# Attention's maxima: split and transposed by VectorE in blocks of 32x32, where TensorE and ScalarE did it through a bank of PSUM

## The chip, the cores and the metric

The kernel runs on one core of one Trainium2 chip. The metric is the device time of one execution in microseconds. The engines are named as the profile names them: PE (TensorE; PEld are its weight loads), DVE (VectorE), ACT (ScalarE), POOL (GpSimd) and SP (SyncE, which only issues DMAs here).

## The reference

One transformer block on a sequence of 2048 rows of 576 values, all in float32. The modulation vectors come from a small product with the condition `c`. The step that matters is attention with 32 heads of 18 values each:

```python
def _A_ref(x, wqkv, wo):
    B, S, D = x.shape
    H = 32; Dh = D // H
    qkv = (x @ wqkv).reshape(B, S, 3, H, Dh).transpose(2, 0, 3, 1, 4)
    q, k, v = qkv[0], qkv[1], qkv[2]
    scores = jnp.einsum("bhqd,bhkd->bhqk", q, k) * Dh ** -0.5
    p = _softmax(scores, axis=-1)
    o = jnp.einsum("bhqk,bhkd->bhqd", p, v)
    return o.transpose(0, 2, 1, 3).reshape(B, S, D) @ wo
```

Around it stand layer norms with modulation, and after it a gated feed-forward part, `(sigmoid(h @ w_gate) * (h @ w_up)) @ w_down` with 4608 hidden values. The inputs `A_wqkv` and `A_wo` are drawn eight times larger than the others, so that the scores are large and the softmax needs the true maximum of each row.

## The kernel before, in words

**Stages.** The first 270 us or so normalise the rows and project queries, keys and values. Then comes attention, up to about 1540 us, with other work woven into it (the weights of the feed-forward part, the output projection of finished rows). The rest is the feed-forward part. The change lies in attention.

**Numbers in two parts.** Products run on values that are split into a high part, which the PE reads exactly (type float32r), and a low part that holds the rest. A query or key head of 18 values therefore takes 54 rows of a tile: high, low and high once more. Two heads lie in one tile, at rows 0 and 64.

**Units and steps.** Attention is 32 units. A unit is two heads and one half of the queries (1024 columns in the tile `q0`, `q1` or `q2`, taken in turn). A unit has 16 steps `kt`, one for each block of 128 keys. In a step the PE makes four blocks of transposed scores (L1084: 128 keys by 512 queries, for two heads and two column halves), ACT takes the exponential of each (L1088), and two steps later the PE multiplies them by the values (L656).

**The maxima.** The exponential needs the maximum of each query's scores. It enters the product as two more rows of the query tile: under the 54 rows of head h stand rows 54 and 55 (64 h + 54 and 64 h + 55), the high and the low part of the negated maximum, and the key tile has ones there. So L1084 reads 56 rows, and the maximum is subtracted inside the product. The maxima are computed about one and a half units ahead: generator `maxima()` makes scores once more with queries on the partitions (L550, 54 rows), in 64 turns for a unit, and DVE reduces each block (L556). Of eight blocks one is passed by ACT through a Relu into `over` (L559) and joined with the next by DVE (L561). After the last turn of a unit, L568 reduces the parts to `nm`, 128 queries by 16 (two heads by 8 blocks of 128 queries), negated.

**Spread.** `nm` has a query on each partition, but the two rows of the query tile have them along one partition. `spread(qs, nm)` carries them over: the PE transposes `nm` into a bank (L581: 16 by 128), ACT copies the bank to float32r, which is the high part (L585), DVE subtracts it from the bank, which gives the low part (L586), and four DMAs on SP (L590) write the rows, one for each head and part, in eight pieces of 512 bytes each. `spread` is a generator: up to its `yield` it issues the transpose, after it the rest.

**Banks.** All scores, transposes and other results in attention take turns in seven banks of PSUM (`bank()`), so an instruction of the PE waits until the reader of the result seven places earlier is done.

**The order of the work.** For PE and ACT the order is written by hand: the context `manual_schedule` names both, and they run in the order of the code. It follows the strings in `STEPS`, one for each pair of steps: `t0` and `t1` are blocks of scores for the exponential (head 0 or 1), `m0`, `m1`, `r0` and `x0` are turns of the maxima (`r0` goes to the Relu, `x0` joins), `V` is a whole product with the values, `A` and `B` its halves, `K` takes a finished output, `O`, `S` and `G` are places where other work starts, and `c` continues what was started. A pair uses the entry of its step number, or `half`; in units 15 to 27 and a half it uses `rows`. Entry 12 is the one with an `S`. When the ninth turn of the next unit's maxima comes, `state["spread"]` is set; that is in the pair at `kt` 12, and the spread then starts at the pair's `S` (or `G`) and goes on at its `c`. The spread of the first unit lies in the projections. DVE, POOL and SP are put in order by the framework's planner: it walks through the program with its own estimate of durations, takes for each engine the first instruction in the order of the code that is ready, and may so put a later one ahead. Within an engine the order is then fixed.

**SP.** On its queue stand, in this part of the program, the DMAs of the spread and the loads of queries and keys for a later unit (`load_heads`, L514 to L522), which are issued at the start of a unit. The maxima of the next unit must have landed in the query tile before that unit's first `L1084`.

Of the kernel before, what the change touches and what calls it, by code (L numbers as in the profile page):

```python
# [23 lines left out]
P = 128  # L24
# [34 lines left out]
}  # L59
ORDERED = 7  # L60
SEVENS = NB - 2
# [26 lines left out]
def tile_block(ctx, tc, x_in, wqkv, wo, w_gate, w_up, w_down, c_in, w_mod, out):  # L88
# [437 lines left out]
    def maxima():  # L526


        n = HW // P
        last = None  # L530
        for u in range(UNITS):
            qs, ks = heads(u)
            mx = mxs[u % 2]
            if u not in SINGLE and u - 2 in SINGLE:
                nc.gpsimd.memset(mx[:, 0:n, 1], LOWEST)
            for i in range(8 * n):
                if last is not None and i == (9 if u == 1 else 8):
                    if u == 1:
                        for _ in spread(*last):
                            pass  # L540
                    else:
                        state["spread"] = last
                qt = i // 8
                pairs = u not in SINGLE
                h, kc = state.get("at") or MAXIMA[i % 8]
                rows = slice(64 * h, 64 * h + 3 * DH)
                paired = pairs and h == 0 and kc < 2
                at = NCH if paired and kc == 0 else kc
                sp = bank()
                nc.tensor.matmul(  # L550
                    sp, qs[rows, qt * P : (qt + 1) * P],
                    ks[rows, at * 512 : (at + 1) * 512], start=True, stop=True,
                )
                to = mx[:, h * n + qt, kc : kc + 1]
                if not paired:
                    nc.vector.tensor_reduce(to, sp, axis=AX.X, op=ALU.max)  # L556
                elif kc == 0:
                    over = small.tile([P, 512], F32, name="over", bufs=1)
                    nc.scalar.activation(over, sp, AF.Relu)  # L559
                else:  # L560
                    nc.vector.tensor_tensor_reduce(  # L561
                        out=over, in0=sp, in1=over, scale=1.0, scalar=LOWEST,
                        op0=ALU.add, op1=ALU.max, accum_out=mx[:, h * n + qt, 0:1],
                    )
                if i < 8 * n - 1:
                    yield
            nm = small.tile([P, 2, n], F32, name="nm")
            nc.vector.tensor_reduce(  # L568
                nm.rearrange("p h t -> p (h t)"), mx, axis=AX.X, op=ALU.max, negate=True
            )  # L570
            last = (qs, nm)
            yield
        for _ in range(8):
            yield
        state["spread"] = last

    def spread(qs, nm):

        n = HW // P
        tp = bank()[0 : 2 * n, 0:P]  # L580
        nc.tensor.transpose(tp, nm.rearrange("p h t -> p (h t)"), ident)  # L581
        yield
        mrows = small.tile([32 + 2 * n, P], F32R, name="mrows", bufs=1)
        parts = [mrows[32 * l : 32 * l + 2 * n] for l in range(2)]
        nc.scalar.copy(parts[0], tp)  # L585
        nc.vector.tensor_sub(parts[1], tp, parts[0].bitcast(F32))  # L586
        for h in range(2):
            for l, part in enumerate(parts):
                to = 64 * h + 3 * DH + l
                nc.sync.dma_start(  # L590
                    qs[to : to + 1, :].rearrange("l (t q) -> l t q", q=P).bitcast(F32),
                    part[n * h : n * (h + 1), :].bitcast(F32),
                )

    todo = maxima()
# [443 lines left out]
    for u in range(UNITS):  # L1039
# [6 lines left out]
        for kt in range(NT):  # L1046
            step = u * NT + kt
            turns["to"] = 64 + 4 * LEAD + 8 * (step // 2 + 1)
            kcols = slice(kt * P, (kt + 1) * P)
            if kt % 2 == 0:  # L1050
                heavy = state.get("next") == "g"
                hold = heavy and (kt == 2 or kt == 12 and u < UNITS - 1)
                halved = step >= 10 and (hold or not heavy)
                rows = FROM0 <= step < FROM1
                order = two_steps(STEPS["full" if not halved else "rows" if rows else kt if kt in STEPS else "half"])
            probs = [None] * 4
            for does, h, c in order[kt % 2]:
                if does == "m":
                    turn(h, c)
                elif does == "K":  # L1060
                    taken()
                elif does in "OSG":
                    if halved and kt == 2:
                        follow.append(outputs())
                        next(follow[-1], None)
                    if "spread" in state:
                        follow.append(spread(*state.pop("spread")))
                        next(follow[-1])
                    if does == "G" and step >= FROM0 and not hold:
                        state["next"] = next(rows0 if step < FROM1 else rows1, None)  # L1070
                elif does == "c":
                    for _ in range(len(follow)):
                        work = follow.pop(0)
                        if next(work, "done") != "done":
                            follow.append(work)
                elif does == "V":
                    if step >= LAG:
                        values()
                elif does in "AB":
                    values(slice(0, 256) if does == "A" else slice(256, 512))  # L1080
                else:
                    sT = bank()
                    rows = slice(64 * h, 64 * h + 3 * DH + 2)
                    nc.tensor.matmul(  # L1084
                        sT, ks[rows, kcols], qs[rows, c * 512 : (c + 1) * 512], start=True, stop=True
                    )
                    pr = probs[2 * c + h] = ppool.tile([P, 512], F32, name=f"p{2 * c + h}")
                    state["exp"] = nc.scalar.activation(pr, sT, AF.Exp, scale=SCALE)  # L1088
            pending.append((half, p, kt, probs))
            if u in (1, 3):  # L1090
                if kt == 0:
                    a = big.tile([P, 8, 640], F32, name="big")
                    a = a.rearrange("p a b -> p (a b)")[:, 0 : 8 * D].rearrange("p (t c) -> p t c", t=4)
                    b = slots.tile([P, 2560], F32, name="w0")[:, 0 : 2 * D]
                    mods = load_mod(a, b, 1 + u // 2)
                    row = slots.tile([P, 2560], F32, name="w1")[:, 0:544]
                    weighed = weigh(mods)
                elif kt >= 5:
                    next(weighed, None)
            elif u in (2, 4) and kt in (2, 4):  # L1100
                takes = [(ga_b, None), (mcol2[:, 1, :], 0.0)] if u == 2 else [(mcol2[:, 0, :], 1.0), (gb_b, None)]
                if kt == 2:
                    weighed = modulate(row, mods[:1], HALVES, takes)
                next(weighed, None)
            if 4 * NT + 8 <= step < FROM0 and step % 4 != 3:
                next(downs, None)
            if step == FROM0:
                for _ in downs:
                    pass
            if step == FROM1 - 1:  # L1110
                for _ in rows0:
                    pass
                bgs.close()
                rawst = ExitStack()
                raws = rawst.enter_context(tc.tile_pool(name="raws", bufs=1, side="right"))
            if u == 30 and kt == 7:
                first = [load_block(raws, b, k, paced) for b, k in ((0, 0), (0, 1), (1, 1))]
            if u >= 30 and kt == 2:
                load_x(u - 30, f"k{u - 30}")
            if u == UNITS - 1 and kt == 3:  # L1120
                nc.sync.dma_start(oend[:, :, 0 : D - DL - 2 * DH], Os[1][:, :, DL : D - 2 * DH])
            if u == UNITS - 1 and kt == 9:
                for _ in rows1:
                    pass
                load_x(2, "w0")
                load_x(3, "w1")
                both = big.tile([P, 2, 5, 512], F32R, name="big")
                for i in range(2):
                    X[5 + i] = both[:, i]
                    load_x(5 + i)  # L1130
# [687 lines left out]
```

## Time and profile before

| | us |
|---|---|
| median of the runs (3 runs, 2797.94 to 2798.35) | 2798.32 |
| the profiled execution | 2804.88 |
| span of its instructions | 2803.1 |
| attention, units 0 to 14 (about) | 267 to 831 |
| attention, units 15 to 31 (about) | 831 to 1540 |

A row of the groups reads: line, engine, operation, what it writes and reads, shapes and count, then durations. In the timeline the first number is the start in us, the second the time taken, and the brackets give the idle time before the instruction and what ended it. `PEld` rows are weight loads; the load of a product waits for what the product waits for, so its start tells when the PE could go on. In the table by stretches each row has the stretch, its length, and the busy time of PE, PEld, DVE, ACT and POOL with the count of instructions, then PE's granted clock, the busy share of the DMA engines, and GB/s.

### The profile page before, as it was taken

What the parts mean: (1) busy time and instruction counts of PE and PEld (TensorE: products, weight loads), DVE (VectorE), ACT (ScalarE), POOL (GpSimd) and SP (SyncE); (2) the same over time, 40 slices, a digit from 0 to 9 for tenths busy, and PEclk for the clock granted to TensorE, in tenths of its full rate; (3) what the DMA queues carried; (4) which work ended last, traced back from release to release, by engine and by line L of the source; (5) the groups of instructions that cost most, each with busy time, mean ns of one, the idle gap of its engine ahead of it and who ended that gap; (6) DMA issues with size and microseconds to landing.
All of it is one profiled execution on the core that took longest, in us unless ns stands there. A gap on an engine that the chain in (4) does not pass through costs nothing.

```text
span 2803.1 us, 50644 instructions
## 1 busy us (share of the span) xinstructions
PE 2771.9 (99%) x18637; PEld 1847.4 (66%) x18637; DVE 2306.3 (82%) x4370; ACT 1609.3 (57%) x3051; POOL 814.6 (29%) x1077
## 2 busy tenths in 40 slices
PE   7999999999999999999999999999999999999999
PEld 5975444444444444444444888888888888888888
DVE  7278999999998888999883778888898677777777
ACT  3215999999999878999888332333333222222221
POOL 3125207888843111663103222232221100000000
PEclk9999999999999999999999999999999999999999
DMA  5344224444432120232127766667767956566653
GB/s 172 121 157 140 78 61 162 171 169 166 172 133 82 36 58 24 98 106 71 43 68 227 273 222 223 240 213 273 278 245 280 339 195 201 194 200 195 200 195 120
DMA packets 170777, 462.59 MB, mean 165 GB/s; under 512 B 21212, under 2 KB 88032, under 8 KB 160416
## 3 DMA queue, kind: packets, MB, share of 16 engines
q1 hardware_dynamic: 150064, 360.72, 38.4%
q0 software_dynamic: 20464, 98.62, 9.9%
q8 instruction: 147, 2.41, 0.4%
q14 instruction: 102, 0.84, 0.1%
HBM read 281.92 MB, written 176.82 MB: 164 GB/s over the span
## 4 chain that ended last, share of the span: by engine, by line
PE 92%; DVE 4%; DMA 2%; issue 2%; POOL 0%; ACT 0%; SPq 0%; DVEq 0%; ACTq 0%; POOLq 0%
PE x L1225 26%; PE o L656 19%; PE s L1084 12%; PE s L550 11%; PE d L1375 8%; PE d L1307 6%; PE s L336 4%; PE s L805 2%; PE s L389 1%; DMA out_dram<-Oa 1%; DVE mx L556 1%; PE s L683 1%; DMA wq_raw<-in_A_wqkv_dram 1%; DVE w L1215 0%; DVE Oa L1379 0%
## 5 line engine op out<-in xcount | busy, mean ns | idle before, releaser
L1088 ACT ACTIVATE p<-s 128x512 f32<-128x512 f32 x2048 | 1069.1, 616 | 89.2 <-PE s L1084 62.6
L556 DVE TENSOR_REDUCE mx<-s 128x1 f32<-128x512 f32 x1568 | 1000.9, 683 | 101.3 <-PE s L550 75.1
L656 PE MATMUL o<-p,vaug 128*32 128x256 f32 (+1 forms) x5848 | 595.1, 478 | 0.1
L550 PE MATMUL s<-k,q 54*128 54x512 f32 x1920 | 548.6, 434 | 2.0 <-DVE t L775 1.0
L1084 PE MATMUL s<-q,k 56*128 56x512 f32 x1920 | 527.7, 440 | 0.0
L550 PEld LDWEIGHTS s<-k,q 54*128 54x128 f32 x1920 | 273.4, 184 | 231.9 <-DVE mx L561 88.0
L1084 PEld LDWEIGHTS s<-q,k 56*128 56x128 f32 x1920 | 249.8, 184 | 232.1 <-ACT p L1088 72.9
L1225 PE MATMUL x<-k,w 128*128 128x512 f32 x1512 | 370.0, 392 | 0.0
L1225 PEld LDWEIGHTS x<-k,w 128*128 128x128 f32 x1512 | 276.8, 188 | 53.3 <-PE o L656 0.8
L1375 PE MATMUL d<-wd,hh 128*128 128x288 f32 x1248 | 249.9, 295 | 2.4 <-DVE Oa L1379 2.4
L656 PEld LDWEIGHTS o<-p,vaug 128*32 128x32 f32 x5848 | 116.2, 108 | 203.1 <-issue 187.5
L1225 PE MATMUL x<-big,w 128*128 128x512 f32 x1008 | 245.5, 392 | 0.7 <-DVE u L1724 0.7
L1225 PE MATMUL x<-w,w 128*128 128x512 f32 x1008 | 245.3, 391 | 0.0
L1225 PEld LDWEIGHTS x<-big,w 128*128 128x128 f32 x1008 | 185.1, 188 | 37.0 <-DVE u L1724 1.1
L1225 PEld LDWEIGHTS x<-w,w 128*128 128x128 f32 x1008 | 184.3, 188 | 34.5
L1375 PEld LDWEIGHTS d<-wd,hh 128*128 128x128 f32 x1248 | 202.2, 188 | 6.2 <-DVE Oa L1379 3.1
L1375 PE MATMUL d<-wd,hl 128*128 128x288 f32 x624 | 184.3, 295 | 0.0
L1379 DVE TENSOR_TENSOR Oa<-Oa,d 128x288 f32<-128x288 f32 x312 | 136.6, 453 | 55.1 <-PE d L1375 51.2
L561 DVE CUSTOM_DVE_ANT_0 over<-s,over 128x512 f32<-128x512 f32 x240 | 163.9, 683 | 1.3 <-PE s L1084 1.2
L559 ACT ACTIVATE over<-s 128x512 f32<-128x512 f32 x240 | 145.8, 608 | 11.3 <-PE s L550 9.3
L1234 ACT ACTIVATE sg<-x 128x512 f32<-128x512 f32 x36 | 21.6, 599 | 210.2 <-PE x L1225 210.2
L1206 ACT CAST w<-S 128x768 fp32r<-128x768 f32 x71 | 59.4, 836 | 137.8 <-POOL S L1179 136.0
(275 smaller groups left out, 3898.5 us busy)
## 6 DMA issues: line engine op xcount, KB each, us to landing
ws<-w SPq DMA_DIRECT2D x126, 640.0 KB
w<-ws SPq DMA_DIRECT2D x126, 640.0 KB
wd<-wds SPq DMA_DIRECT2D x19, 1152.0 KB
k<-kd SPq DMA_DIRECT2D x60, 360.0 KB
wds<-w POOLq DMA_DIRECT2D x18, 1152.0 KB, 5.2
wtd<-t POOLq DMA_DIRECT2D x32, 576.0 KB, 5.0
wt<-wtd SPq DMA_DIRECT2D x64, 288.0 KB
wd<-wds SPq DMA_DIRECT2D x52, 288.0 KB
```

The source lines that it names most:

```text
L336: nc.tensor.matmul(acc, w, hT[:, t, cols], start=n == 0, stop=n == len(ts_) - 1)
L550: nc.tensor.matmul(sp, qs[rows, qt * P : (qt + 1) * P], ks[rows, at * 512 : (at + 1) * 512], start=True, stop=True,)
L556: nc.vector.tensor_reduce(to, sp, axis=AX.X, op=ALU.max)
L559: nc.scalar.activation(over, sp, AF.Relu)
L561: nc.vector.tensor_tensor_reduce(out=over, in0=sp, in1=over, scale=1.0, scalar=LOWEST, op0=ALU.add, op1=ALU.max, accum_out=mx[:, h * n + q ...
L656: nc.tensor.matmul(acc[32 * j : 32 * j + 32, cols], vaug[:, kt, (2 * p + h) * VW : (2 * p + h) * VW + 32], probs[2 * c + h][:, cols], star ...
L1084: nc.tensor.matmul(sT, ks[rows, kcols], qs[rows, c * 512 : (c + 1) * 512], start=True, stop=True)
L1088: state["exp"] = nc.scalar.activation(pr, sT, AF.Exp, scale=SCALE)
L1225: nc.tensor.matmul(acc[v], w[:, v, a, :], X[s][:, b, :], start=first and n == 0, stop=n == 6, skip_group_check=not first,)
L1307: nc.tensor.matmul(acc, a[:, rows], w[:, k, :], start=n == 0, stop=n == 2)
L1375: nc.tensor.matmul(acc[:, :HALF], a[:, f, rows], w[:, f, cols], start=n == 0, stop=n == 5)
L1379: nc.vector.tensor_add(Oa[:, t, cols], Oa[:, t, cols], acc[:, :HALF])
```

## The change

`spread` no longer uses the PE, ACT or a bank. DVE copies `nm` into the high part of a tile `split` (128 by 32: head, part, block) and subtracts it for the low part, then transposes `split` in four separate blocks of 32 by 32 into `mrows`. In block `a` (partitions 32 a to 32 a + 31) the rows are head, part and block of 128 queries, and the 32 columns are the queries 32 a to 32 a + 31 of each block. Eight DMAs, one for each block `a` and head, write both rows of the head: 2 by 8 pieces of 128 bytes each. `spread` is now a plain function that issues everything at one place, the pair's `G`; the entry for `kt` 12 in `STEPS` and the letter `S` are gone, so that pair takes the usual order `half`.

```diff
@@ STEPS
-    12: "V t0m1 m0t1 m1t0 S A c r0t1 m1t0 G B c t1t0 m1x0 t1m0",
@@ maxima()
                 if last is not None and i == (9 if u == 1 else 8):
                     if u == 1:
-                        for _ in spread(*last):
-                            pass
+                        spread(*last)
@@ spread(qs, nm)
         n = HW // P
-        tp = bank()[0 : 2 * n, 0:P]
-        nc.tensor.transpose(tp, nm.rearrange("p h t -> p (h t)"), ident)
-        yield
-        mrows = small.tile([32 + 2 * n, P], F32R, name="mrows", bufs=1)
-        parts = [mrows[32 * l : 32 * l + 2 * n] for l in range(2)]
-        nc.scalar.copy(parts[0], tp)
-        nc.vector.tensor_sub(parts[1], tp, parts[0].bitcast(F32))
-        for h in range(2):
-            for l, part in enumerate(parts):
-                to = 64 * h + 3 * DH + l
+        split = small.tile([P, 4 * n], F32R, name="split", bufs=1)
+        hi, lo = (split.rearrange("p (h l t) -> p h l t", h=2, l=2)[:, :, l, :] for l in range(2))
+        nc.vector.tensor_copy(hi, nm)
+        nc.vector.tensor_sub(lo, nm, hi.bitcast(F32))
+        mrows = small.tile([P, 4 * n], F32R, name="mrows", bufs=1)
+        nc.vector.transpose(mrows.bitcast(F32), split.bitcast(F32))
+        for a in range(4):
+            for h in range(2):
+                to, p0 = 64 * h + 3 * DH, 32 * a + 2 * n * h
                 nc.sync.dma_start(
-                    qs[to : to + 1, :].rearrange("l (t q) -> l t q", q=P).bitcast(F32),
-                    part[n * h : n * (h + 1), :].bitcast(F32),
+                    qs[to : to + 2, :].rearrange("l (t a q) -> l t a q", a=4, q=32)[:, :, a, :].bitcast(F32),
+                    mrows[p0 : p0 + 2 * n, :].bitcast(F32),
                 )
@@ the loop over units and steps
-                elif does in "OSG":
+                elif does in "OG":
                     ...
                     if "spread" in state:
-                        follow.append(spread(*state.pop("spread")))
-                        next(follow[-1])
+                        spread(*state.pop("spread"))
```

## The prediction

> **What bounds the kernel now.** I read the page first, then the busy time of each engine over single pairs of attention steps, then the starts of TensorE's weight loads, then VectorE, SyncE and the lines of the edit.
>
> ```profile
> span 2803.1 us, 50644 instructions
> PE 2771.9 (99%) x18637; PEld 1847.4 (66%) x18637; DVE 2306.3 (82%) x4370; ACT 1609.3 (57%) x3051; POOL 814.6 (29%) x1077
> ```
>
> The average says TensorE and nothing else. The edit lies in attention alone, so I cut four neighbouring pairs out of unit 12, from one Relu to the next; the columns are length, then busy time of PE, PEld, DVE, ACT and POOL. Below them stand the two halves of attention.
>
> ```profile
> 719.35:723.98 4.63, 4.63 (x42) 2.05 (x40) 4.35 (x9) 4.54 (x11) 4.63 (x8) 1.00 0.28 116
> 723.98:728.61 4.63, 4.63 (x42) 2.00 (x40) 4.39 (x10) 4.56 (x11) 4.55 (x8) 1.00 0.00 0
> 728.61:733.44 4.83, 4.83 (x43) 2.03 (x41) 4.68 (x9) 4.72 (x11) 4.83 (x9) 1.00 0.31 126
> 733.44:738.20 4.76, 4.76 (x42) 2.02 (x40) 4.49 (x10) 4.52 (x11) 3.52 (x6) 1.00 0.81 286
> ...
> 267.00:831.00 564.00, 564.00 (x4781) 242.12 (x4779) 524.11 (x991) 548.38 (x1099) 341.19 (x534) 1.00 0.40 138
> 831.00:1500.00 669.00, 666.00 (x5316) 295.90 (x5314) 583.35 (x1130) 592.76 (x1179) 203.62 (x278) 1.00 0.22 68
> ```
>
> In the first half all three engines are nearly full: in an ordinary pair of 4.63 us ACT works 4.54 to 4.56 and DVE 4.35 to 4.39, which leaves DVE 0.24 to 0.28 us. In the second half DVE idles 669.00 - 583.35 = 86 us. So an instruction taken from ACT or PE should show in the first half, and one given to DVE is not free there.
>
> **What the step costs now.** These are weight loads at the first score of each pair, in unit 12 with the transpose's own load, and of three pairs in unit 21, the last with the transpose.
>
> ```profile
> 721.95 0.18 PEld L1084 LDWEIGHTS s<-q,k 56*128 56x128 f32 x1 [0.84 <-ACT p L1088]
> 726.56 0.18 PEld L1084 LDWEIGHTS s<-q,k 56*128 56x128 f32 x1 [0.84 <-ACT p L1088]
> 731.23 0.18 PEld L1084 LDWEIGHTS s<-q,k 56*128 56x128 f32 x1 [0.84 <-ACT p L1088]
> 732.13 0.09 PEld L581 LDWEIGHTS s<-ident,nm 128*16 128x16 f32 x1 [0.25 <-issue]
> 736.20 0.18 PEld L1084 LDWEIGHTS s<-q,k 56*128 56x128 f32 x1 [0.84 <-ACT p L1088]
> ```
>
> ```profile
> 1109.12 0.18 PEld L550 LDWEIGHTS s<-k,q 54*128 54x128 f32 x1 [0.18 <-ACT p L1088]
> 1113.80 0.18 PEld L550 LDWEIGHTS s<-k,q 54*128 54x128 f32 x1 [0.18 <-ACT p L1088]
> 1118.63 0.18 PEld L550 LDWEIGHTS s<-k,q 54*128 54x128 f32 x1 [0.20 <-ACT p L1088]
> ```
>
> Unit 12: two pairs of 4.61 and 4.67 us, mean 4.64, then the pair with the transpose, 736.20 - 731.23 = 4.97: an excess of 0.33 us. Unit 21: 4.68, then 4.83: an excess of 0.15. There are 32 spreads. One lies in the projections; 15 lie in units 0 to 14, and 16 in units 15 to 30.
>
> **Removed.** The group rows of the four instructions (duration lowest, median, highest in ns):
>
> ```profile
> L581 PE MATMUL s<-ident,nm x32: 276/277/278, 215.9 to 1487.3; 128*16 128x128 f32 x32
> L585 ACT CAST mrows<-s x32: 237/239/256, 216.2 to 1488.7; 16x128 fp32r<-16x128 f32 x32
> L586 DVEq EVENT_SEMAPHORE  x60: 49/50/50, 269.4 to 1485.2; - x60
> L586 DVE TENSOR_TENSOR mrows<-s,mrows x32: 279/280/283, 216.7 to 1488.9; 16x128 fp32r<-16x128 f32 x32
> L590 SPq DMA_DIRECT2D q<-mrows x128: 620/630/1506, 216.5 to 1491.0; - x128
> ```
>
> The excess of 0.33 us is what 0.28 of PE, 0.24 of ACT and the DVE subtraction cost together; they overlap, so I take the measured excess and not their sum. The special order goes too, and the pair is then ordered as its three predecessors, whose 4.64 us is what I measure against. Gain if nothing came in place: 15 x 0.33 = 5.0 and 16 x 0.15 = 2.4, together 7.4 us. The bank that the transpose took is free as well; that is inside the excess.
>
> **Added on VectorE.** Copy, subtract and transpose, over 16, 16 and 32 elements, each needing the one before. No row shows a DVE transpose or a copy this small. The nearest rows are small dependent operations in attention:
>
> ```profile
> 1079.38 1.28 DVE L556 TENSOR_REDUCE mx<-s 128x1 f32<-128x512 f32 x2
> 1080.58 0.16 DVE L228 TENSOR_SCALAR sd<-sd 128x8 f32<-128x8 f32 x1
> 1080.65 0.68 DVE L561 CUSTOM_DVE_ANT_0 over<-s,over 128x512 f32<-128x512 f32 x1
> ...
> 1082.05 0.17 DVE L226 TENSOR_TENSOR sd<-r 128x8 f32<-128x8 f32 x1
> 1082.25 0.17 DVE L227 TENSOR_TENSOR sd<-sd,var 128x8 f32<-128x8 f32 x1
> 1082.45 0.17 DVE L228 TENSOR_SCALAR sd<-sd 128x8 f32<-128x8 f32 x1
> ```
>
> Alone between two big reductions such an operation moves the next one by 0.07 us (1080.65 - 1080.58). In a chain each takes 0.20 us (1082.05, 1082.25, 1082.45). So three cost 0.21 us at least and 0.60 at most. Against DVE's 0.24 us of room the lower end costs the pair nothing, and the upper 0.36. The Trainium skill ("VectorE: DVE Perf Modes", section "Rules for kernel authors") says that chaining VectorE operations saves nothing and that their number should be kept small; that speaks against one operation becoming three. By it the sum would take the chain's end; the row with 0.07 us disagrees with it where a long reduction stands on either side.
>
> Which end applies depends on where the planner puts them, since VectorE's order is not written by hand. It does move work ahead of its place in the code: statistics of tile 0 are emitted after all eight tiles are projected, yet in the trace they follow the first tile's addition by half a microsecond:
>
> ```profile
> L209 DVE BATCH_NORM_STATS2 st<-Oa x16: 460/460/463, 885.6 to 1068.8; 128x6 f32<-128x288 f32 x16
> L807 DVE TENSOR_TENSOR Oa<-t,s x16: 453/454/457, 885.1 to 1068.3; 128x288 f32<-128x288 f32 x16
> ```
>
> So I expect the three to run as soon as VectorE is free behind the maxima's own reduction, not at the point G, 6.6 us later:
>
> ```profile
> 727.14 0.22 DVE L568 TENSOR_REDUCE nm<-mx 128x16 f32<-128x64 f32 x1
> 727.28 3.25 DVE L556 TENSOR_REDUCE mx<-s 128x1 f32<-128x512 f32 x5
> ...
> 733.72 0.28 DVE L586 TENSOR_TENSOR mrows<-s,mrows 16x128 fp32r<-16x128 f32 x1
> ```
>
> I choose two of them chained behind that reduction and the third between others: 0.20 + 0.20 + 0.07 = 0.47 us, less 0.24 of room = 0.23 us in each of 15 units, 3.5 us. In the second half I take 0.05 us in 16 units, 0.8 us, with ends of 0 (DVE has room) and 0.15 (the excess is eaten). Added: 4.3 us, with ends 0 and 15 x 0.36 + 16 x 0.15 = 7.8 us.
>
> **Added on SyncE.** Eight issues in place of four, in pieces of 128 bytes in place of 512.
>
> ```profile
> 308.92 2.76 SPq L590 DMA_DIRECT2D q<-mrows  x4
> 733.48 2.75 SPq L590 DMA_DIRECT2D q<-mrows  x4
> 739.45 0.79 SPq L514 DMA_DIRECT2D q<-qd  x1
> ```
>
> Four take 2.75 us, so eight take 5.5. Behind them on SP stands the next load of heads, at 739.45; started at the old place, the eight end at 739.0, so it is not held up. TensorE waits for up to four more DMA semaphores before a unit's first score. At 0.05 us for a wait instruction (the EVENT_SEMAPHORE row above) that is 0.2 us, hidden under the value product that runs there for 1.07 us (next fence); uncovered it would be 6 us in all. I cost both at nothing. What the longer queue could do is the third rival.
>
> **The sum.** Gain 7.4 less 4.3 = 3.1 us. The profiled execution took 2804.9 us (span 2803.1), so this one would take 2801.8; the runs' median stands 6.6 us below it, so I forecast 2798.3 - 3.1 = 2795.2 us. Its own range is 2790.9 (nothing added) to 2798.7 (7.8 added).
>
> **Rivals.** First, *all three fall into idle time of VectorE*: 2798.3 - 7.4 = 2790.9 us. For it speaks the 0.07 us row and the planner's habit; against it, that the five reductions behind the maxima's reduction (727.28, 3.25 us) run without a gap, so that what is put ahead of them delays them all.
>
> Second, *VectorE becomes the bound of its pair*: a chain of 0.60 us directly behind that reduction holds the banks of those five, and TensorE, which needs them, passes the whole delay on with no room deducted. 15 x (0.60 - 0.33) = 4.1 and 16 x (0.30 - 0.15) = 2.4 give 2804.8 us. It decides where more than 0.33 us reaches TensorE. Against it: the reduction itself (0.22 us) stands in the second pair above, 4.67 us long, hardly more than its neighbour.
>
> Third, on the other side, *the maxima's rows arrive late*. The next unit's first score reads them:
>
> ```profile
> 739.80 1.07 PE L656 MATMUL o<-p,vaug 128*32 128x512 f32 x8
> 741.14 0.65 PE L1084 MATMUL s<-q,k 56*128 56x512 f32 x3
> ...
> 312.00:312.50 0.50, 0.50 (x6) 0.17 (x2) 0.50 (x2) 0.32 (x1) 0.00 (x0) 1.00 0.04 8
> 312.50:313.00 0.50, 0.50 (x10) 0.16 (x8) 0.50 (x2) 0.50 (x2) 0.00 (x0) 1.00 0.00 0
> ...
> x1p<-t POOLq DMA_DIRECT2D x8, 288.0 KB, 2.4
> ```
>
> In a quiet unit (2) the last issue ends at 308.92 + 2.76 = 311.68 and DMA traffic is gone by 312.50, 0.8 us later; a DMA issued by POOL lands 2.4 us after its start, or 1.8 after 0.63 of issue. So today's four, issued by 736.23, are there at 737.0 to 738.0 and have 3.1 to 4.1 us to spare. Four more take 2.75 of it and the shorter pair 0.1 to 0.3. The first issue may therefore start 0.1 to 1.2 us later than today's 733.48, no more; from there each microsecond costs one in 31 units. If the planner leaves the chain at G, it begins where the subtraction stands now (733.72) and ends at 734.3 in one piece, on the edge. With a reduction of 0.60 us between each two it ends at 735.5, some 1.2 us too late: 31 x 1.2 = 37, or 2835 us. Against it: the chain can start at 727.3, six microseconds sooner.
>
> **How the numbers follow.** A measurement of this kernel can tell about 0.2%, 5.6 us, from no change: below 2792.7 is faster, above 2803.9 slower. Forecast 0.47, first rival 0.28, second 0.10, third 0.15. The forecast lies within 0.2%; the first rival is faster; the second straddles the upper bound and is halved; the third is slower. With 0.02 of the forecast's tail on the faster side: faster 0.30, same 0.50, slower 0.20. The range runs from 2789.5, a little under the first rival, whose excesses are read from single pairs, to 2806, over the second; the third is left out, and with the first's tail that is 2 in 10.
>
> **What would show it.** Right: no transpose and no small copy in the pair at kt 12, which shrinks to 4.64 us in units 0 to 14; the three VectorE operations stand within a pair of the maxima's reduction, 0.2 us each where chained; the pair at kt 10 grows by 0.2 us; SP issues eight, the first before 733.5 in unit 12's terms. Wrong: a gap of ACT at the first exponential of each unit that a DMA ends (third rival); a pair at kt 10 longer by 0.5 us (second); no pair longer at all (first); a DVE transpose far outside 0.16 to 0.28 us, or an issue far from 0.63 us, would break the terms themselves.

## The result, and the profile after

The changed kernel takes 2822.75 us (median of 4 runs, 2820.28 to 2827.44), against 2798.13 us of the kernel before beside it (2795.52 to 2798.35): a ratio of 1.0092, with a 95% interval from 1.0075 to 1.011. It is slower by some 25 us, and the prediction of 2795.2 us was wrong: the time lies above its range of 2789.5 to 2806. The profiled execution took 2820.65 us, against 2804.88.

The page of the kernel after, its span and the busy time of the engines:

```profile
span 2818.9 us, 50811 instructions
PE 2773.1 (98%) x18605; PEld 1844.3 (65%) x18605; DVE 2327.2 (83%) x4434; ACT 1606.9 (57%) x3019; POOL 814.6 (29%) x1077
```

DVE has 20.9 us more than before (2306.3). Three operations of 0.2 us in 32 units would be 19 us, less the 9 us (32 x 0.28) of the subtraction that went; so half of it is something else. PE, which lost 32 products, is busy a microsecond longer.

**Where the time went.** The busy time by stretches, of before and then of after: two pairs of unit 14, those at `kt` 10 and 12, and then units 1 to 14 and units 15 to 30 as a whole, each from the first exponential of its first unit. The columns are stretch, length, and busy time of PE, PEld, DVE, ACT and POOL, then the granted clock.

```profile
803.67:808.35 4.68, 4.68 (x42) 1.96 (x41) 4.52 (x10) 4.55 (x10) 0.00 (x0) 1.00 0.64 257
808.35:813.30 4.95, 4.95 (x43) 2.20 (x42) 4.66 (x9) 4.71 (x10) 0.00 (x0) 1.00 0.02 4
279.05:818.43 539.38, 539.38 (x4576) 231.90 (x4573) 501.34 (x948) 524.36 (x1052) 331.29 (x522) 1.00 0.41 140
818.43:1496.44 678.01, 675.11 (x5392) 299.71 (x5388) 593.52 (x1149) 601.73 (x1197) 206.37 (x281) 1.00 0.22 69
```

```profile
811.78:816.87 5.09, 5.02 (x42) 2.05 (x41) 4.87 (x13) 4.55 (x9) 0.00 (x0) 1.00 0.58 235
816.87:821.47 4.60, 4.60 (x42) 1.88 (x40) 4.38 (x8) 4.52 (x10) 0.00 (x0) 1.00 0.02 3
274.92:826.63 551.71, 542.76 (x4562) 230.79 (x4562) 511.25 (x976) 523.59 (x1037) 331.27 (x522) 0.99 0.40 137
826.63:1516.97 690.34, 681.54 (x5376) 302.42 (x5370) 602.98 (x1181) 600.18 (x1181) 206.15 (x281) 0.99 0.22 67
```

Both halves of attention are 12.3 us longer, 24.7 together, as much as the medians differ: the whole loss lies there. (The two profiled executions differ by 15.8 us only, because the one of before was 8.9 us longer outside these units.) The pair at `kt` 12 did shrink, 4.95 to 4.60 us. The pair at `kt` 10 grew, 4.68 to 5.09 us in unit 14, where POOL is idle. Cut the same way in every unit, the pair at `kt` 12 gives back 5.2 us over units 1 to 14 and 3.3 over units 15 to 30; the other pairs are as before in the mean, within 0.05 us, except those at `kt` 10. These grew by 1.24 us in the mean of units 1 to 14 and by 0.96 in units 15 to 30, and most unevenly: by 0.4 us in units 1, 3, 4 and 14, 1.4 in unit 11, 6.6 in unit 2. In all they grew by 32.6 us.

**What stands in that pair.** The new instructions of VectorE (duration lowest, median, highest in ns), with the maxima's own reduction:

```profile
L566 DVE TENSOR_REDUCE nm<-mx x32: 209/220/222, 205.2 to 1502.4; 128x16 f32<-128x64 f32 x32
L580 DVE CAST split<-nm x32: 165/175/4477, 209.2 to 1502.7; 128x16 fp32r<-128x16 f32 x32
L581 DVE TENSOR_TENSOR split<-nm,split x32: 167/176/3529, 209.4 to 1502.9; 128x16 fp32r<-128x16 f32 x32
L583 DVE STREAM_TRANSPOSE mrows<-split x32: 195/202/214, 209.6 to 1503.6; 128x32 f32<-128x32 f32 x32
```

The medians are what the prediction assumed. But one copy took 4.48 us and one subtraction 3.53, for the same 16 elements; the transpose and the reduction hardly vary. Here is VectorE in unit 1 and in unit 2, then POOL in unit 2:

```profile
298.73 0.17 DVE L580 CAST split<-nm 128x16 fp32r<-128x16 f32 x1
298.94 0.18 DVE L581 TENSOR_TENSOR split<-nm,split 128x16 fp32r<-128x16 f32 x1
...
338.58 4.48 DVE L580 CAST split<-nm 128x16 fp32r<-128x16 f32 x1
343.09 0.17 DVE L581 TENSOR_TENSOR split<-nm,split 128x16 fp32r<-128x16 f32 x1
```

```profile
337.54 2.78 POOL L142 TENSOR_TENSOR big<-big 128x576 f32<-128x576 f32 x2
340.28 2.74 POOL L142 TENSOR_TENSOR big<-big,w 64x576 f32<-64x576 f32 x2
```

The copy of unit 2 starts in the middle of four POOL instructions that run without a gap, and it ends at 343.06, 0.04 us after the last of them (340.28 + 2.74 = 343.02). It is the same throughout: of the 64 copies and subtractions 21 took longer than 0.24 us, and 20 of these end 0.02 to 0.04 us after the end of a POOL instruction; the 36 that took their 0.17 us with no POOL instruction under way at their start are the undisturbed ones, and the other seven met only the last 0.2 us of one, or a POOL instruction that issues a DMA. In all, copy and subtraction took 15.8 and 14.5 us where 64 x 0.175 = 11.2 would have done: 19.1 us of waiting.

The pairs at `kt` 10 of units 2, 11, 15, 22 and 25, with the granted clock in the column before the last two:

```profile
338.28:349.58 11.30, 7.13 (x42) 2.50 (x42) 9.30 (x13) 4.77 (x9) 5.50 (x5) 0.70 0.17 54
694.75:700.81 6.06, 5.17 (x42) 2.04 (x41) 5.84 (x13) 4.70 (x9) 4.41 (x7) 1.00 0.58 201
850.68:858.35 7.67, 6.58 (x44) 2.52 (x40) 6.08 (x12) 4.79 (x11) 4.91 (x6) 0.78 0.15 40
1162.04:1173.18 11.14, 7.07 (x44) 2.56 (x41) 9.32 (x12) 4.76 (x10) 9.26 (x10) 0.69 0.14 51
1288.14:1297.24 9.10, 7.47 (x40) 2.53 (x32) 6.69 (x12) 4.77 (x10) 8.66 (x11) 0.66 0.19 69
```

In unit 11 the pair grew, beyond the 5.09 us of a unit without a stretch, by 0.97 us, and the copy had stretched by 0.98: the delay is passed on and no more. In unit 2 the stretch is 4.30 us and the pair grew by 6.2. There, and in units 15, 22 and 25, the clock granted to TensorE fell as well. In those three the stretches of copy and subtraction together are 1.5, 4.4 and 2.1 us, and an undisturbed pair is 4.77 us long (units 21, 24 and 26); so the surplus over the stretch is 1.9, 1.4, 2.0 and 2.2 us in units 2, 15, 22 and 25, 7.5 us in all. The clock fell in a fifth place, the pair at `kt` 12 of unit 20 (half rate from 1089.63 to 1093.04 us), which is 1.0 us longer than before although neither operation was stretched there; the cause of that one stays open, and its microsecond is already taken off the 3.3 us above.

**The rows of the maxima** were not late. SP's eight issues in unit 1, and TensorE's load at unit 2's first score, which needs them:

```profile
301.66 5.37 SPq L587 DMA_DIRECT2D q<-mrows  x8
```

```profile
312.33 0.19 PEld L1080 LDWEIGHTS s<-q,k 56*128 56x128 f32 x2
```

The last issue ends at 307.03, five microseconds ahead of the first score, and no unit's first score waits for a DMA on these rows.

### The profile page after: what moved, and what is told of

It reads as the page before. It is cut to its first block, busy times and chain, and to the rows that moved or that the text cites. A ratio compares the mean times of both kernels' runs of the same rounds, so it can differ in the third digit from the quotient of the medians.

```text
span 2818.9 us, 50811 instructions
## 1 busy us (share of the span) xinstructions
PE 2773.1 (98%) x18605; PEld 1844.3 (65%) x18605; DVE 2327.2 (83%) x4434; ACT 1606.9 (57%) x3019; POOL 814.6 (29%) x1077
## 4 chain that ended last, share of the span: by engine, by line
PE 90%; DVE 7%; issue 2%; POOL 1%; ACT 0%; DMA 0%; SPq 0%; DVEq 0%; ACTq 0%; POOLq 0%
PE x L1221 27%; PE o L653 18%; PE s L1080 11%; PE s L548 10%; PE d L1371 8%; PE d L1303 6%; PE s L335 4%; DVE mx L554 2%; PE s L802 2%; PE s L388 1%; PE s L680 1%; DVE over L559 1%; DVE split L580 0%; DVE w L1211 0%; DVE Oa L1375 0%
## 5 line engine op out<-in xcount | busy, mean ns | idle before, releaser
L548 PE MATMUL s<-k,q 54*128 54x512 f32 x1920 | 556.0, 439 | 1.0 <-DVE t L772 1.0
```

The source lines that it names most:

```text
L548: nc.tensor.matmul(sp, qs[rows, qt * P : (qt + 1) * P], ks[rows, at * 512 : (at + 1) * 512], start=True, stop=True,)
```

## The experiments

Two theories went in. **Theory A**: the copy and the subtraction, by their form, wait for a POOL instruction that is under way. **Theory B**: any operation put behind the maxima's reduction delays the pair, VectorE being its bound, and the form does not matter. Medians stand beside the median of the kernel before from the same set of runs. In the diffs `...` stands for lines left out.

### Reductions in place of copy and subtraction

```diff
@@ maxima()
-nm = small.tile([P, 2, n], F32, name="nm")
-nc.vector.tensor_reduce(
-    nm.rearrange("p h t -> p (h t)"), mx, axis=AX.X, op=ALU.max, negate=True
-)
+both = small.tile([P, 8 * n], F32R, name="split", bufs=1)
+part = both.rearrange("p (c h l t) -> p l h t c", c=2, h=2, l=2)
+by4 = mx.rearrange("p (h t) k -> p h t k", h=2)
 ...
+nc.vector.tensor_reduce(part[:, 0, :, :, 1].bitcast(F32), by4, axis=AX.X, op=ALU.max)
+nc.vector.tensor_reduce(part[:, 0, :, :, 0], by4, axis=AX.X, op=ALU.max, negate=True)
+nc.vector.tensor_reduce(part[:, 1, :, :, 0], part[:, 0].bitcast(F32), axis=AX.X, op=ALU.add, negate=True)
 ...
@@ spread()
 ...
-nc.vector.tensor_copy(hi, nm)
-nc.vector.tensor_sub(lo, nm, hi.bitcast(F32))
 ...
```

> The changed kernel with its copy and its subtraction replaced by reductions: one writes the plain maxima, one writes their negated, rounded part straight from the eight maxima of a unit, one sums the two, negated, to give the rest. DVE still runs four small operations per unit, all with a single SBUF input; transpose and DMAs are as in the changed kernel. Theory A (the copy and the subtraction wait until a running POOL instruction ends): no small operation is stretched, the longest stays under 0.3 us; the 19 us of stretch leave and the time comes to 2800 to 2807 us, 16 to 22 below the changed kernel's 2822.7. Theory B (VectorE is the bound of its pair, whatever the form): as many operations, each a little longer, so 2822 to 2826 us, and the kt-10 pair stays at 5.1 us or more everywhere.

Measured: 2794.16 us against 2798.88, a ratio of 0.9981 (0.9972 to 0.9989). The four small operations, and one unit in which POOL is at work through two of them:

```profile
L569 DVE TENSOR_REDUCE split<-mx x32: 206/220/222, 205.9 to 1475.1; 128x16 f32<-128x64 f32 x32
L570 DVE TENSOR_REDUCE split<-mx x32: 206/208/211, 206.1 to 1475.2; 128x16 fp32r<-128x64 f32 x32
L571 DVE TENSOR_REDUCE split<-split x32: 174/186/191, 206.9 to 1475.5; 128x16 fp32r<-128x32 f32 x32
L584 DVE STREAM_TRANSPOSE mrows<-split x32: 195/199/213, 210.0 to 1476.2; 128x32 f32<-128x32 f32 x32
```

```profile
1185.15 0.21 DVE L570 TENSOR_REDUCE split<-mx 128x16 fp32r<-128x64 f32 x1
1185.39 0.19 DVE L571 TENSOR_REDUCE split<-split 128x16 fp32r<-128x32 f32 x1
```

```profile
1184.89 1.29 POOL L846 TENSOR_TENSOR ho<-t,ho 128x512 fp32r<-128x512 f32 x1
```

Theory B falls: with as many operations, in the same places, 28.6 us are gone, even more than the 16 to 22 that theory A expected (it counted the stretch and not what the clock took). Of the 96 reductions 34 ran wholly while a POOL instruction was under way, and none took more than 0.222 us. The version is 0.19% faster than the kernel before, too. Its pair at `kt` 10 is 5.00 to 5.02 us in every one of units 1 to 14, so 0.34 us are left that have nothing to do with POOL.

### One added operation at a time

Each of these is the kernel before with one more instruction in each unit, whose output (in a tile `extra`, of which `hi` and `lo` are halves) nobody reads. First the copy:

```diff
 ...
+nc.vector.tensor_copy(hi, nm)
```

> The kernel before with one more VectorE instruction per unit, whose output nobody reads: the copy of the 128x16 negated maxima within SBUF. Theory A: its median is near 0.17 us but single ones reach 1 to 4 us where POOL is at work; 32 copies with 10 us of stretch in all, and the time goes to 2806 to 2813 us. Theory B: one operation more costs 0.07 to 0.20 us in the busy units, 1 to 5 us in all, 2799 to 2803 us, and no copy takes more than 0.3 us.

Measured: 2813.39 us against 2798.88, a ratio of 1.0048 (1.0036 to 1.0061).

Then a subtraction of two SBUF inputs:

```diff
 ...
+nc.vector.tensor_sub(lo, nm, nm)
```

> The kernel before with one more VectorE instruction per unit, whose output nobody reads: a subtraction of two SBUF inputs, 128x16. Theory A, if a second SBUF input is enough to wait for POOL: stretched as the copy was (median 0.17, single ones 1 to 4 us), 2807 to 2816 us. If only the copy's form waits and the subtraction was stretched for another reason: none over 0.3 us, 2799 to 2803 us.

Measured: 2814.55 us against 2800.24, a ratio of 1.0052 (1.0039 to 1.0064).

And a transpose:

```diff
 ...
+nc.vector.transpose(extra, mxs[0].rearrange("p h k -> p (h k)")[:, 0 : 4 * n])
```

> The kernel before with one more VectorE instruction per unit, whose output nobody reads: a transpose of a 128x32 tile within SBUF, in 32x32 blocks. Theory A: with a single SBUF input it never waits for POOL, each takes 0.20 us, and the kernel is 1 to 5 us longer, 2799 to 2803 us. Theory B says the same of its time; if the transpose is stretched like the copy, theory A's reading of which forms wait is wrong.

Measured: 2801.66 us against 2798.88, a ratio of 1.0013 (1.0004 to 1.0022). The added instruction of the three kernels:

```profile
L582 DVE CAST extra<-nm x32: 159/174/4345, 209.8 to 1493.6; 128x16 fp32r<-128x16 f32 x32
```

```profile
L582 DVE TENSOR_TENSOR extra<-nm x32: 161/176/4277, 210.2 to 1495.8; 128x16 fp32r<-128x16 f32 x32
```

```profile
L581 DVE STREAM_TRANSPOSE extra<-mx x32: 198/201/213, 206.1 to 1437.2; 128x32 f32<-128x32 f32 x32
```

The copy alone and the two-input subtraction alone are each stretched to more than 4 us, in the same unit 2, and each costs 14 to 15 us, the copy a little over the upper end expected. The transpose, the longest of the three by its median, is never stretched, although nine of its 32 ran wholly while a POOL instruction was under way, and it costs under 3 us. The form decides. The undisturbed copy also answers a point of the prediction: it takes 0.17 us, and the pairs with it are 4.87 us in place of 4.67, so all of it reaches TensorE. The transpose added 0.09 us to the pair at `kt` 10 in the odd ones of units 1 to 14; in the even ones the planner put it into the pair at `kt` 12, which it made 0.12 us longer.

### The other side: POOL idle

```diff
@@ weigh
-                nc.gpsimd.tensor_scalar(part, part, sc[:k, t : t + 1], 0.0, op0=ALU.mult, op1=ALU.add)
 ...
-                    nc.gpsimd.tensor_tensor(whole, whole, part, op=ALU.add)
+                    pass
```

> The changed kernel without the scaling and summing of modulation weights by POOL in units 0, 2 and the like (so it leaves out a part of the computation, the modulation product of those weights). In the changed kernel this POOL work ran without a gap while the copy of unit 2 waited 4.48 us. Theory A: with POOL idle there, that copy takes 0.17 us and the pair of unit 2 is 5.1 us in place of 11.3; the one of unit 22, whose POOL work is other, stays at 11 us; the time falls by 5 to 8 us, to 2815 to 2818 us. Theory B: the pair of unit 2 stays near 11 us and the time at 2822.

Measured: 2812.23 us against 2800.24, so 10.5 us under the changed kernel (12.6 by the distances of the two to the kernel before). Copy and subtraction, and the pairs at `kt` 10 of units 2 and 22:

```profile
L579 DVE CAST split<-nm x32: 165/175/1249, 210.4 to 1493.0; 128x16 fp32r<-128x16 f32 x32
L580 DVE TENSOR_TENSOR split<-nm,split x32: 166/176/3532, 210.6 to 1493.2; 128x16 fp32r<-128x16 f32 x32
```

```profile
340.13:345.22 5.09, 5.04 (x42) 2.04 (x41) 4.87 (x13) 4.55 (x10) 0.00 (x0) 1.00 0.01 2
1153.60:1165.02 11.42, 7.30 (x44) 2.55 (x40) 9.35 (x12) 4.78 (x10) 9.54 (x11) 0.70 0.14 50
```

With POOL's work gone, unit 2's pair is an undisturbed one; unit 22, whose POOL work stayed, keeps its 11 us. The time fell by more than expected because the pairs of units 0, 15 and 25 lost 0.9, 2.9 and 0.9 us too.

### Stalls of six lengths, without waits for POOL

```diff
+stalls["n"] += 1
+r = {3: 8, 5: 16, 7: 32, 9: 48, 11: 64, 13: 80}.get(stalls["n"] - 1)
 ...
+nc.vector.tensor_reduce(
+    extra, nm.rearrange("p h t -> p (h t)").unsqueeze(2).to_broadcast([P, 2 * n, 4 * r]),
+    axis=AX.X, op=ALU.max,
+)
```

> The kernel before with one reduction of a single SBUF input, whose output nobody reads, behind the maxima's own in six units: 512, 1024, 2048, 3072, 4096 and 5120 elements long per partition, about 0.6, 1.1, 2.2, 3.3, 4.3 and 5.4 us, in units 2, 4, 6, 8, 10 and 12. In the changed kernel a stretch of 0.98 us lengthened its pair by 0.97, but 2.1 us by 4.35, 4.31 by 6.2 and 4.38 by 6.45. Theory C (TensorE, once it has idled some microseconds, is granted a lower clock for a while, which makes the loss more than the stall): the pairs grow by the reduction's own length up to 1.1 us, and by 1.4 to 2.3 us more than it from 2.2 us on, with a granted clock under 0.95 in those stretches alone; in all 17 us of reductions cost 22 to 26 us, so 2821 to 2825 us. Rival D (the surplus came from POOL's locked port or from what the planner put behind): each pair grows by its reduction's length within 0.4 us, 2813 to 2817 us.

Measured: 2827.21 us against 2800.24, 27.0 more. The six pairs at `kt` 10, from unit 2 on:

```profile
337.66:343.04 5.38, 5.17 (x42) 2.04 (x42) 5.10 (x10) 4.70 (x10) 5.08 (x5) 1.00 0.01 3
416.76:422.68 5.92, 5.16 (x42) 2.03 (x41) 5.64 (x11) 4.70 (x9) 2.47 (x4) 1.00 0.00 1
494.55:502.80 8.25, 6.48 (x42) 2.39 (x42) 6.73 (x11) 4.75 (x9) 8.25 (x14) 0.79 0.24 101
574.69:584.76 10.07, 7.24 (x42) 2.57 (x42) 7.86 (x10) 4.76 (x9) 4.14 (x7) 0.66 0.69 264
656.65:667.30 10.65, 6.73 (x42) 2.50 (x41) 8.95 (x11) 4.75 (x10) 10.57 (x18) 0.68 0.01 2
739.18:751.62 12.44, 7.47 (x42) 2.75 (x42) 10.00 (x11) 4.75 (x10) 7.53 (x13) 0.73 0.62 238
```

| reduction, us | 0.69 | 1.22 | 2.29 | 3.35 | 4.42 | 5.49 |
|---|---|---|---|---|---|---|
| pair over 4.67 us | 0.71 | 1.25 | 3.58 | 5.40 | 5.98 | 7.77 |
| surplus | 0.02 | 0.03 | 1.29 | 2.05 | 1.56 | 2.28 |

Theory C holds, and rival D falls. Up to 1.2 us the pair grows by the stall and no more than 0.03 us on top; from 2.3 us on, 1.3 to 2.3 us come on top, in the pairs whose clock fell and in no others. The whole is a microsecond over the expected 22 to 26; in the profiled execution units 1 to 14 are 24.4 us longer than before. TensorE's own idle time is shorter than the stall: 0.70 us at the stall of 1.22, where the clock stayed at 1.00, and 1.77 us in the third of these pairs, where the clock was halved a microsecond after TensorE had gone on:

```profile
497.78 0.50 PE L1094 MATMUL s<-q,k 56*128 56x512 f32 x2 [1.77 <-DVE mx L556]
```

```profile
499.00:500.00 1.00, 1.00 (x6) 0.55 (x4) 1.00 (x2) 0.92 (x2) 1.00 (x3) 0.50 0.00 0
```

### The order of the pair alone

```diff
-    12: "V t0m1 m0t1 m1t0 S A c r0t1 m1t0 G B c t1t0 m1x0 t1m0",
```

> The kernel before with the usual order at kt 12 alone: the transpose by TensorE, ACT's copy and the four DMAs stay, but are issued at G in place of S. Under both theories the order is a small term: 2797 to 2803 us, with the pair at kt 12 between 4.9 and 5.2 us. If it comes out more than 10 us above the kernel before, the order and not VectorE's operations is behind the loss, and both theories fall.

Measured: 2798.92 us against 2798.88, a ratio of 0.9999 (0.999 to 1.0007). The pair at `kt` 12 is 5.05 us in place of 4.96 in units 1 to 14; the order plays no part in the loss.

### Eight issues at the old place

```diff
-        for h in range(2):
+        for h in [0, 1, 0, 1]:
             for l, part in enumerate(parts):
```

> The kernel before with its four DMAs of the maxima's rows issued twice, so eight issues on SP at the old place, the same bytes written again. The prediction's third rival put the margin of the rows at 3.1 to 4.1 us and four more issues at 2.75 us: so no first score waits, 2797 to 2801 us. If the margin is smaller than read, each microsecond late costs 31 us in all: over 2805 us.

Measured: 2814.83 us against 2800.24, a ratio of 1.0051 (1.0039 to 1.0064), far above the 2797 to 2801 expected. The group row of the first scores, with what ended their waits:

```profile
L1084 PE MATMUL s<-q,k 56*128 56x512 f32 x1920 | 534.3, 442 | 6.7 <-DMA q<-mrows 4.4 <-DVE mx L556 1.6 <-ACT over L559 0.7
```

In the quiet unit 2 the margin is enough: the eight end at 309.93 us and the unit's first score, at 311.98, waits for nothing. But in units 7 and 14, where other transfers are under way, the first pair is 8.8 us long in place of 4.4, at a granted clock of 0.61; in units 6, 10, 11, 13 and 16 it is 0.7 to 1.5 us longer. The DMA engines are busy for 0.56 and 0.54 of the two long pairs. The first pairs of units 1 to 14 make up 13.1 of the 14.6 us.

### The copy on ACT

```diff
-        nc.vector.tensor_copy(hi, nm)
+        nc.scalar.copy(hi, nm)
```

> The changed kernel with the copy made by ACT, whose place is the pair's G, written by hand; the subtraction and the transpose stay on VectorE and now come behind it, at kt 12. So the DMAs of the rows start at the old place, eight of them. From the run with the four DMAs issued twice (14.6 us) the late rows cost about 15 us, and they start about a microsecond later than there, so 15 to 35; kt 10 loses its chain (8 to 30 us back), the subtraction keeps its waits for POOL (5 to 9 us). If both hold: 2808 to 2835 us, with first scores of units that wait for a DMA on the rows. If the planner's early place in the changed kernel was worth nothing, no first score waits and the time is 2795 to 2805.

Measured: 2822.19 us against 2800.39, a ratio of 1.0084 (1.0067 to 1.0101). SP in unit 7, and TensorE's load at the first score of unit 8:

```profile
543.59 5.36 SPq L587 DMA_DIRECT2D q<-mrows  x8
```

```profile
552.65 0.42 PEld L1080 LDWEIGHTS s<-q,k 56*128 56x128 f32 x2 [2.94 <-issue]
```

Both parts hold. The pair at `kt` 10 is back at 4.67 us. The rows now end their issue at 548.95 and the last of them lands at 552.67, when the score begins, after 2.66 us in which TensorE multiplied nothing; in units 7, 11 and 14 it idles for 0.9 to 1.8 us ahead of the first score, and the first pairs of most others grow by 0.1 to 0.5. The subtraction still reaches 2.28 us where POOL is at work, now at `kt` 12.

### Copy and subtraction on POOL

```diff
-        nc.vector.tensor_copy(hi, nm)
-        nc.vector.tensor_sub(lo, nm, hi.bitcast(F32))
+        nc.gpsimd.tensor_copy(hi, nm)
+        nc.gpsimd.tensor_sub(lo, nm, hi.bitcast(F32))
```

> The changed kernel with copy and subtraction given to POOL; VectorE only transposes. No VectorE instruction can then wait for POOL's port, but the transpose stands in VectorE's order one reduction behind the maxima's and must wait for POOL's two. Where POOL is free that is 0.3 to 1 us in the pair at kt 10; in units 2 and 22, where POOL is at work for 4 to 5 us, the pair at kt 10 is 9 to 12 us, as in the changed kernel. 2800 to 2830 us. If POOL were always free in time: 2788 to 2794 us, below the version with reductions.

Measured: 2915.63 us against 2800.39, a ratio of 1.0412 (1.0397 to 1.0428), far beyond the range. POOL and VectorE in unit 0:

```profile
270.10 2.75 POOL L142 TENSOR_TENSOR big<-big,w 64x576 f32<-64x576 f32 x2
272.79 0.20 POOL L580 CAST split<-nm 128x16 fp32r<-128x16 f32 x1
```

```profile
273.33 0.21 DVE L583 STREAM_TRANSPOSE mrows<-split 128x32 f32<-128x32 f32 x1 [12.87 <-POOL split L581]
```

POOL takes only 0.2 us for the copy, but its order is fixed, and the copy stands behind other work that is not done yet: VectorE stands still for 12.87 us here and 95.6 us in 17 units. At 16 places POOL stands still too, 111.7 us in all, with the copy next in its order and `nm` not ready. The expected bound, the length of one run of POOL work, was the wrong one; what counts is how far the two engines are apart in the orders that the planner fixed for them.

## Why the prediction was wrong

**What held.** The gain was read rightly: the pair at `kt` 12 fell to 4.59 us in units 1 to 14 and the second half gave 0.2 us a unit, together some 8.5 us where 7.4 was forecast. The planner did move the copy and the subtraction directly behind the maxima's reduction and the transpose among the reductions after it. The transpose's 0.202 us was inside the stated 0.16 to 0.28. An issue took 0.61 us, and SP and the further waits cost nothing. The third rival, late rows, did not come, because the issue starts 10.7 us ahead of the first score (301.66 and 312.33 above).

**The step that failed** is the cost of the operations added on VectorE, "0.21 us at least and 0.60 at most" in a pair. The upper end was taken from a chain that ran alone, and was used as if nothing could lengthen an operation of 16 elements. The copy and the subtraction took up to 4.5 and 3.5 us, because they wait for POOL. The term "Added: 4.3 us" came out as 32.6 us in the pairs at `kt` 10. By the runs: the gain of 8.5 us stands against some 7 us of undisturbed cost (0.42 us in 14 units, 0.08 in 16) and some 26 us of waiting, 19 of stretch and 7.5 of lowered clock by the rows above; the run with reductions, which has neither, is 28.6 us below.

The Trainium skill states the mechanism ("SBUF — State Buffer", section "Who interferes with whom"): VectorE's second pair of ports is shared with GpSimd under an exclusive lock; a copy in a two-port mode, or an instruction with two SBUF inputs beside a GpSimd one that reads SBUF, blocks until the other ends, and a reduction never contends on this chip. The traces agree on which forms wait: copy and two-input subtraction alone were stretched to 4.3 us each, and the reductions took 0.222 us at the longest. That the copy ran in a two-port mode is not shown by any run here. The prediction named a page on VectorE that speaks of the count of operations, and not this one.

The trace of before could have told. Two rows of it, from the start of the kernel, VectorE and POOL:

```profile
52.82 1.25 DVE L226 TENSOR_TENSOR sd<-r 128x4 f32<-128x4 f32 x1 [1.12 <-POOL r L223]
```

```profile
52.75 1.30 POOL L363 TENSOR_TENSOR kd_d<-pl 128x512 f32<-128x512 f32 x1
```

This is the instruction whose 0.17 us at 1082.05 the prediction quoted as its price. Here it takes 1.25 us and ends with POOL's; at 1082 POOL was idle, so the rows chosen could not show it. The old subtraction, L586, read one input from PSUM and was 283 ns at the longest; that difference of form was in the diff.

**The room of 0.24 us** was also wrong, as a smaller term. It was deducted from the cost, but a copy of 0.17 us lengthens its pair by 0.20, and a stall of 0.69 us by 0.71: nothing is absorbed. The 0.07 us for an operation between others was small too: the transpose alone cost 0.09 to 0.12. The second rival had the room right ("TensorE passes the whole delay on with no room deducted"), though it priced the chain at 0.60 us where 0.42 was passed on. VectorE's idle time in the pair does not lie behind the maxima's reduction, where five more follow without a gap. What the change would take with POOL out of the way no run shows. An estimate: in the version with reductions the pairs at `kt` 12 gave back 10.7 us and those at `kt` 10 cost 6.0, which is its 4.7 us; with the 7 us of copy and subtraction some 1 to 4 us would be left, by the gain of 8.5 or of 10.7. So the forecast of 3.1 us less was not far off for a VectorE that nobody holds up, in part because a gain and a cost that were both put too low offset each other.

**The third rival's margin** was too wide, though it was not called on. It was read from a quiet unit as 3.1 to 4.1 us, with 2.75 us for four more issues; at the old place they cost 14.6 us, in the units in which other transfers are under way.

## What to carry to other kernels

Before a VectorE operation of PSUM is moved to SBUF, ask by its form (a copy, or two SBUF inputs) whether it will wait for POOL, and look at what POOL runs at that place: the rest of the instruction under way is the least price, a whole run of POOL instructions the highest seen here, and the row to read is the highest duration of such forms in the trace, not the median. Reductions and a transpose did the same work here without waiting. A stall of VectorE that TensorE has to sit through cost its own length up to 1.2 us, and 1.3 to 2.3 us more from 2.3 us on; in between, at 1.08 and 1.85 us of idle time of TensorE, it went either way.

## What the runs showed of the hardware

**How long such an operation waits.** Of the 21 stretched copies and subtractions 17 waited for the rest of one POOL instruction only, and 12 of these got through although POOL's next one (in two cases the issue of a DMA) followed without a gap. But the copy of unit 2 waited through four in a row, 4.48 us, and so did the subtraction of unit 22, 3.53 us. The copy and the subtraction that were added alone to the kernel before waited through four in unit 2 as well (4.35 and 4.28 us). What decides between one and four stays open.

**When TensorE's clock falls.** Two rows of TensorE, from unit 15 of the changed kernel and from the first score of unit 11 with the copy on ACT:

```profile
852.63 0.50 PE L1080 MATMUL s<-q,k 56*128 56x512 f32 x1 [1.08 <-DVE mx L554]
```

```profile
674.27 0.70 PE L1080 MATMUL s<-q,k 56*128 56x512 f32 x2 [1.85 <-issue]
```

After the idle time of 1.08 us the clock was at half rate from 854.11 to 857.52; after 1.85 us it stayed at 1.00. So the length of one gap does not settle it. The records of the clock show a grid: in the changed kernel and in the run with the stalls each lowered stretch in attention is 3.41 or 6.83 us long, and their starts lie whole multiples of 3.41 us apart within a run. Where a gap falls in that grid may be what decides, but no run here tests it. The Trainium skill ("TensorE: Matmul & The Clock Gate", section "What's actually happening") has half clock after an idle window of about 3.4 us; the half rate is what the trace shows (0.50), but gaps of 1.77 and 1.08 us brought it here.
